# Conversion of 64-bit weights to 32 bits: the exponent test on ScalarE, one mask on VectorE, the integer sum last on GpSimd

## The chip, the cores and the metric

The kernel runs on one core of a Trainium2 chip. The core has a matrix engine (TensorE, in the rows PE, with its weight loads as PEld), VectorE (DVE), ScalarE (ACT), GpSimd (POOL) and SyncE (SP), which issues most DMA transfers. Each engine works through its own queue in order; semaphores tie them together. The metric is the device time of one execution in microseconds, lower is better.

## The reference

Three networks run one after the other: attention with local and global tokens, a top-1 mixture of eight experts, and a gated feed-forward network. The change lies in the preparation of the third one's weights.

```python
def _moe_ref(x, w_gate, w_local, w1, w2):          # the experts
    ...                                            # per token an expert e: its own best, or the one before it
    h = np.maximum(x[b, s] @ w1[e], 0.0)
    out[b, s] = p[e] * (h @ w2[e])

def _moe2_ref(x, w_in, conv_w, w_out):             # the "second network" of the kernel's feed-forward part
    h = np.maximum(x @ w_in, 0.0)
    ...                                            # conv_out: 3 taps of conv_w along the sequence
    gate = 1.0 / (1.0 + np.exp(-conv_out))
    return (h * gate @ w_out).astype(np.float32)
```

`w_in` (512 x 1024), `w_out` (1024 x 512) and `conv_w` (3 x 1024) come as 64-bit floats. The kernel reads each number as two 32-bit words and makes a 32-bit float of it with integer operations: the sign and exponent moved by three bits, the mantissa rounded, and zero where the exponent is too small.

## The kernel before, in words

The order of instructions on every engine is that of the Python code (a manual schedule). After attention, tokens are sorted into slots of at most 128 tokens of one expert. `Moe.run` goes through the slots with `step(s)`; step s does, in this order:

- `layer1(s)`: 24 matmuls of 128x512 into `hp` (the expert's first layer in three products of high and low parts), then two ReLU copies on ACT into `hs`. A slot with few tokens (`few_l1`) uses small matmuls and one short ReLU.
- `fetch(s, 1)`: load of the next first-layer weights if the expert changes. `gather` of the slot after next but one.
- `turn_x(s + 1)`: four transposes on PE (L1353) into `xlp`, ACT's cast to `xh` (L1363), DVE's difference `xl` (L1103).
- the closing operation of the conversion that the step before began (`self.conv.pop()()`, its instruction is L1019 on DVE).
- `raw_load`: SP's load of the next raw chunk (L1481) into one of two halves of `fx`.
- `resplit(s + 1, 1)`: if the expert changes, ACT casts the new weights to `wh` (L1045) and DVE makes `wl` (L1046), inside a branch whose end is L1331. `layer1` of the next slot waits for that end on DVE whether the expert changes or not.
- `convert`, the early place (L1457), if the next slot's expert does not change.
- `layer2(s - 1)`: 24 matmuls into `yp` (L1126), the copy to `ys` on ACT (L1438, or L1413 with few tokens), a scatter on POOL.
- `turn_h(s)`: eight transposes (L1424), two casts to `gh` on ACT (L1425), two differences `gl` on DVE (L1103); with few tokens only L1401 and one copy (L1402).
- `resplit(s, 2)`: the second-layer weights, eight `wh` and eight `wl` of 128x512.
- `convert`, the late place (L1471), if the next slot's expert changes.

So each of the 16 chunks (128 x 512 numbers) is converted once, in steps 3 to 18, early or late; a conversion of `conv_w` (24 x 128 numbers) follows after step 19. Before, a conversion is six DVE operations (L1012 to L1017), a sum on POOL (L1018), and one DVE operation that is put off to the next step (L1019): an XOR and the AND with the exponent test. `wf` holds the converted chunks; they are used when all slots are done (`split`, `split_out`).

Of the kernel before, what the change touches and what calls it, by code (L numbers as in the profile page):

```python
# [8 lines left out]
F32 = mybir.dt.float32  # L9
# [993 lines left out]
POOL_F = ()  # L1003
DVE_F = (1, 3, 5, 7)
POOL_K = {1: (), 2: ()}


def conv64(nc, raw, out):
    hi, lo = raw[:, :, 1], raw[:, :, 0]
    v = nc.vector  # L1010
    a = out.bitcast(I32)
    v.tensor_scalar(a, hi, 3, 0x7FFFFFFF, ALU.logical_shift_left, ALU.bitwise_and)  # L1012
    v.scalar_tensor_tensor(a, hi, -2 ** 31, a, ALU.bitwise_and, ALU.bitwise_or)
    v.tensor_scalar(hi, hi, 1, 21, ALU.logical_shift_left, ALU.logical_shift_right)
    v.tensor_scalar(hi, hi, 897.0, -1.0, ALU.is_ge, ALU.mult)
    v.scalar_tensor_tensor(a, lo, 29, a, ALU.logical_shift_right, ALU.bitwise_or)
    v.tensor_scalar(lo, lo, 28, 1, ALU.logical_shift_right, ALU.bitwise_and)  # L1017
    nc.gpsimd.tensor_tensor(a, a, lo, ALU.add)  # L1018
    return lambda: v.scalar_tensor_tensor(a, a, 0x40000000, hi, ALU.bitwise_xor, ALU.bitwise_and)  # L1019


class Weights:
# [28 lines left out]


class Moe:
    def __init__(self, sig, tc, W, ident, x_dram, y_dram, rt, w1, w2, wi, wo):
        self.nc, self.tc = tc.nc, tc
        self.W, self.ident, self.x_dram, self.y_dram = W, ident, x_dram, y_dram
        self.rt, self.w1, self.w2, self.wi, self.wo = rt, w1, w2, wi, wo
        self.sig = sig
        self.xs, self.xt, self.ht, self.hs, self.next, self.chg, self.sm = {}, {}, {}, {}, {}, {}, {}
        self.conv, self.raw = [], {}  # L1060

    def open(self, ctx):
        self.ctx = ctx
# [123 lines left out]
    def run(self, cw6, cwr, cw, f2):  # L1187
        nc, W, tc = self.nc, self.W, self.tc
        n = NSLOT - 3
        self.f2 = f2  # L1190
        for s in range(NA, n - 1):
            self.step(s)
            if s == NA + 17:
                self.conv.append(conv64(nc, cw6, cwr))
        self.last(n - 1, cwr, cw)
        r = nc.values_load(self.rt.esi[0:1, 4, 1:2], min_val=0, max_val=P + 1)
        with tc.If(r != 0):
            r = nc.values_load(self.rt.esi[0:1, 4, 0:1], min_val=0, max_val=NB)
            with tc.If(r > n - NA):
                for s in range(n, NSLOT):  # L1200
                    self.slot(s)
            f2.load0()
            for i in range(5):
                f2.scale0(i, self.ps)
                f2.xt0(i, self.ps)
        self.split_out()
# [236 lines left out]
    def step(self, s):  # L1443
        W, hi = self.W, NSLOT - 3
        self.small(s + 1)
        self.layer1(s)
        self.fetch(s, 1)
        if s + 3 < hi:
            self.xs[s + 3] = self.gather(s + 3)
        self.turn_x(s + 1)  # L1450
        while self.conv:
            self.conv.pop()()
        if s < NA + 16:
            self.raw_load(s - NA)
        self.resplit(s + 1, 1)
        if NA < s <= NA + 16:
            with self.tc.If(self.chg[s + 1] == 0):  # L1457
                self.convert(s - NA - 1)
        if s == NA:
            for _ in self.rest:  # L1460
                pass
        else:
            self.layer2(s - 1)
            self.fetch(s - 1, 2)
        if s == hi - 2:
            self.f2.load0()
        self.turn_h(s)
        self.resplit(s, 2)
        if NA < s <= NA + 16:
            self.conv.pop()  # L1470
            with self.tc.If(self.chg[s + 1] != 0):  # L1471
                self.convert(s - NA - 1)

# [8 lines left out]

    def convert(self, s):
        n, k, o = self.chunk(s)
        self.conv.append(conv64(self.nc, self.raw[s], self.W.f[n][:, k, o:o + 512]))


class Ffn2:
# [249 lines left out]
def moe_kernel(ctx, tc, q_l, k_l, v_l, q_g, k_g, v_g, w_gate, w_local, w1, w2, w_in, conv_w, w_out, out):  # L1738
    nc = tc.nc
    outf = out.rearrange("b s d -> (b s) d")  # L1740
    with tc.manual_schedule():
# [9 lines left out]
        warm = cp.tile([P, 1], F32, name="warm")  # L1751
        nc.scalar.activation(warm, ident[:, 0:1], AF.Exp)
        L = cp.tile([P, NT, 9], F32, name="L")
        cp.tile([P, PAD_C], F32, name="pad_c")
        cc = Consts()

        def late():
# [22 lines left out]
        def hook(n, end):  # L1780
            if n + end > 20 and (end or todo.get("y") != "pe"):
                for _ in range(STEPS_A[end]):
                    todo["y"] = next(ph, 0)
                    if todo["y"] == "es":
                        todo["load"] = True
                    if todo["y"] in (0, "pe"):
                        break
            if not end:
                return
            if n == N_Y:  # L1790
                nc.sync.dma_start(y_dram[0:S, :], x_dram[0:S, :])
            if n == 25:
                right.close()
                hl = ctx.enter_context(tc.tile_pool(name="w_hl", bufs=1, side="right"))
                st = moe_ctx.enter_context(tc.tile_pool(name="w_x", bufs=1, side="right"))
                W = Weights(nc, hl, st)
                m = todo["m"] = Moe(warm, tc, W, ident, x_dram, y_dram, rt, w1, w2, w_in.bitcast(I32),
                                    w_out.bitcast(I32))
            m = todo.get("m")
            if todo.pop("load", False):  # L1800
                W = m.W
                todo["e0"] = m.reg(nc.sync, 0, 0, E - 1)
                for a in (0, 2):
                    W.load_k(1, w1[bass.ds(todo["e0"], 1)], a, a + 2)
            if m and todo.get("y") == 0 and not m.xs and not m.xt:
                todo["g"] = n
                ca.close()
                todo["xp"] = xa.enter_context(tc.tile_pool(name="m_xa", bufs=1, side="right"))
                for s in range(NA):
                    m.xs[s] = m.gather(s, todo["xp"])  # L1810
            if n - todo.get("g", n) == GATHER_T:
                m.hs0 = todo["xp"].tile([P, FF], F32, name="hs0")
                m.xt[0] = m.hi_lo_t(m.xs.pop(0), NKC, "x", todo["xp"], at.ps)
            for k in SPLIT_W1.get(n, ()):
                m.W.split_k(1, m.W.s, k, nc.gpsimd)
            if n in (30, 31):
                for a in range(2):
                    k = 4 * (n - 30) + 2 * a
                    m.W.load_k(2, w2[bass.ds(todo["e0"], 1)], k, k + 2)
            if n == 32:  # L1820
                cs.close()
                m.psh = moe_ctx.enter_context(tc.tile_pool(name="m_h", bufs=1, space=PSUM, side="right"))
                todo["fill"] = m.fill()
            if n >= 32:
                for _ in range(TAIL[n - 32]):
                    next(todo["fill"])
                for k in SPLIT_W2.get(n, ()):
                    m.W.split_k(2, m.W.s, k, nc.vector)
# [71 lines left out]
```

## Time and profile before

| | us |
|---|---|
| three timed runs | 618.85, 621.88 (median), 623.83 |
| profiled execution, device time | 619.98 |
| its span, first to last instruction | 618.2 |
| PE busy | 571.3 (92% of the span) |
| DVE busy | 407.5 (66%) |
| ACT busy | 308.3 (50%) |
| POOL busy | 173.7 (28%) |

The profile is of one execution. A timeline lists instructions with their start from the first instruction of the program, in microseconds, and in brackets how long the engine was idle before one and what ended that. Matmuls overlap, so their sums exceed the stretch. A windows view gives busy time by engine and the clock that TensorE was granted (1.00 is 2.4 GHz, 0.50 is 1.2 GHz) for stretches of the span.

### The profile page before, as it was taken

To read this page: it belongs to the slowest core of one execution; us is meant where nothing else is said; L and a number is where in the kernel's file an instruction comes from. 1 tells how busy PE (TensorE), PEld (TensorE's weight loads), DVE (VectorE), ACT (ScalarE), POOL (GpSimd) and SP (SyncE) were. 2 spreads that over 40 slices of the span, in tenths; PEclk is the share of its full clock that TensorE was granted. 3 is DMA by queue.
4 is the path that set the end of the run, shared out by engine and by line. 5 is a ranking of instruction groups with operands and counts; after the bars stand their busy time and mean duration, and the time that the engine had idled before them with its cause. 6 is when DMAs were issued, how large, how long until landed. Compare 5 with 4: busy or idle time off the path is not lost. (4 is left out here: it accounts for less than half of the span.)

```text
span 618.2 us, 16382 instructions
## 1 busy us (share of the span) xinstructions
PE 571.3 (92%) x6108; PEld 477.8 (77%) x6108; DVE 407.5 (66%) x854; ACT 308.3 (50%) x623; POOL 173.7 (28%) x226
## 2 busy tenths in 40 slices
PE   7779899888889999989989799979899999999997
PEld 6567677666667888768767688769898998998986
DVE  7868576875974867885687885366864484383330
ACT  5755555565225544652454724547753564463441
POOL 7655830034022423143132431010302313300100
PEclk9998899999999999999999989979899999999999
DMA  9989949568229765576357593322110201000001
GB/s 230 216 184 247 237 114 209 175 216 255 83 64 323 285 228 218 160 282 236 135 177 264 187 319 107 125 83 64 52 36 25 77 18 35 35 0 35 36 35 51
DMA packets 60643, 90.57 MB, mean 147 GB/s; under 512 B 25726, under 2 KB 34198, under 8 KB 60504
## 3 DMA queue, kind: packets, MB, share of 16 engines
q1 hardware_dynamic: 57016, 78.93, 42.1%
q0 software_dynamic: 3520, 10.23, 4.9%
q8 instruction: 65, 1.06, 0.7%
q14 instruction: 42, 0.34, 0.2%
HBM read 125.87 MB, written 15.79 MB: 229 GB/s over the span
## 5 line engine op out<-in xcount | busy, mean ns | idle before, releaser
L1604 DVE SCALAR_TENSOR_TENSOR fc<-f_hp,cw,fc 128x544 f32<-128x544 f32 (+2 forms) x66 | 51.7, 783 | 73.3 <-ACT fc L1602 71.9
L1046 DVE TENSOR_TENSOR wl<-ws,wh 128x512 fp32r<-128x512 f32 (+1 forms) x80 | 64.6, 869 | 8.1 <-ACT wh L1045 6.9
L1045 ACT CAST wh<-ws 128x512 fp32r<-128x512 f32 (+1 forms) x84 | 58.0, 770 | 1.7 <-DMA ws<-in_moe_w_dram 0.7
L1126 PE MATMUL yp<-wh,gh 128*128 128x512 f32 x136 | 54.8, 403 | 0.9 <-ACTq L1331 0.9
L1662 PE MATMUL f<-wh,fh 128*128 128x512 f32 (+1 forms) x144 | 54.8, 381 | 0.0
L1126 PE MATMUL yp<-wl,gh 128*128 128x512 f32 x136 | 53.5, 394 | 1.1 <-DVEq L1331 0.7
L1662 PE MATMUL f<-wh,fl 128*128 128x512 f32 (+1 forms) x144 | 54.4, 378 | 0.0
L1662 PE MATMUL f<-wl,fh 128*128 128x512 f32 (+1 forms) x144 | 54.4, 378 | 0.0
L1126 PE MATMUL yp<-wh,gl 128*128 128x512 f32 x136 | 53.3, 392 | 0.0
L1110 PE MATMUL hp<-wl,xh 128*128 128x512 f32 x136 | 45.5, 407 | 8.4 <-DVEq L1331 5.3
L1083 POOL DMA_INDIRECT y_dram<-ys,sidx x22 | 25.4, 1156 | 86.5 <-ACT ys L1438 38.7
L1309 ACT ACTIVATE hs<-hp 128x512 f32<-128x512 f32 x34 | 18.7, 594 | 61.3 <-PE hp L1110 61.3
L278 ACT ACTIVATE pr<-sp,nm 128x128 f32<-128x128 f32 x128 | 36.6, 376 | 24.7 <-DVE nm L275 24.7
L1110 PE MATMUL hp<-wh,xh 128*128 128x512 f32 x136 | 46.2, 412 | 0.2 <-ACT ys L1413 0.2
L1071 POOL DMA_INDIRECT xs<-x_dram,gidx x22 | 26.9, 1223 | 65.3 <-DMA ws<-in_moe_w_dram 34.0
L1110 PE MATMUL hp<-wh,xl 128*128 128x512 f32 x136 | 44.7, 401 | 0.0
L1018 POOL TENSOR_TENSOR wf<-wf,fx 128x512 int32<-128x512 int32 x16 | 20.9, 1304 | 74.0 <-DVE fx L1017 65.6
L1110 PEld LDWEIGHTS hp<-wl,xh 128*128 128x128 f32 x136 | 25.8, 193 | 15.8 <-DVEq L1331 6.6
L1609 ACT ACTIVATE f_hp<-f 128x544 f32<-128x544 f32 x31 | 19.4, 625 | 37.4 <-PE f L1585 33.4
L1103 DVE TENSOR_TENSOR gl<-hlp,gh 128x512 fp32r<-128x512 f32 x34 | 22.0, 685 | 18.3 <-ACT gh L1425 13.9
L1438 ACT COPY ys<-yp 128x512 f32<-128x512 f32 x15 | 8.9, 591 | 50.0 <-PE yp L1126 47.2
L1671 ACT COPY fy<-f 128x512 f32<-128x512 f32 (+1 forms) x18 | 10.1, 564 | 46.7 <-PE f L1662 46.7
(381 smaller groups left out, 1529.0 us busy)
## 6 DMA issues: line engine op xcount, KB each, us to landing
ws<-in_moe_w_dram SPq DMA_DIRECT2D x42, 2048.0 KB
fx<-y_dram SPq DMA_DIRECT2D x17, 256.0 KB
raw<-in_k_l_dram SPq DMA_DIRECT2D x16, 256.0 KB
x_dram<-x SPq DMA_DIRECT2D x16, 256.0 KB
fx<-in_moe_w_in_dram SPq DMA_DIRECT2D x8, 512.0 KB
fx<-in_moe_w_out_dram SPq DMA_DIRECT2D x8, 512.0 KB
out_dram<-fy SPq DMA_DIRECT2D x16, 256.0 KB
VA<-in_v_l_dram SPq DMA_DIRECT2D x20, 192.0 KB
```

The source lines that it names most:

```text
L278: nc.scalar.activation(pr[:, hp, :], sp[:, hp, :], AF.Exp, bias=nm[:, hp:hp + 1], scale=-1.0)
L1018: nc.gpsimd.tensor_tensor(a, a, lo, ALU.add)
L1045: (cp.tensor_copy if cp else self.nc.scalar.copy)(h, src[n][:, k, :])
L1046: eng.tensor_tensor(l, src[n][:, k, :], h.bitcast(F32), ALU.subtract)
L1071: self.nc.gpsimd.indirect_dma_start(out=xs, out_offset=None, in_=self.x_dram[0:n, :], in_offset=bass.IndirectOffsetOnAxis(ap=self.rt.gidx[ ...
L1083: self.nc.gpsimd.indirect_dma_start(out=self.y_dram[:, :], out_offset=bass.IndirectOffsetOnAxis(ap=self.rt.sidx[:, s:s + 1], axis=0), in_= ...
L1103: self.nc.vector.tensor_tensor(hl[1][:, a:a + 4], t, hl[0][:, a:a + 4].bitcast(F32), ALU.subtract)
L1110: self.nc.tensor.matmul(hp[c], a[:, k, :], b[:, 512 * c:512 * c + 512], start=k == 0 and m == 0, stop=k == NKC - 1 and m == 2)
L1126: self.nc.tensor.matmul(yp, a[:, k, :], b, start=k == 0 and m == 0, stop=k == NFC - 1 and m == 2)
L1604: nc.vector.scalar_tensor_tensor(c[:, a:b], hp[:, a + t:b + t], self.cw[:, t, f:f + 1], c[:, a:b], ALU.mult, ALU.add)
L1609: self.nc.scalar.activation(hp[:, 1:S + 1].rearrange("p (a c) -> p a c", a=2), p[:, :, 0:272], AF.Relu)
L1662: self.nc.tensor.matmul(yp[:, cs], x[:, c], w[:, cs], start=f == 0 and n == 0, stop=f == NFC - 1 and n == 2)
```

## The change

The exponent test goes from DVE to ACT: the high word, read as a 32-bit float, is made positive (`Abs`), compared with the limit `TINY` by `Sign(limit - x)`, and written as an integer: -1, all bits set, where the number is large enough. `m`, one tile for all conversions, is the fifth part of `fx`, which nothing else uses in these steps. On DVE the shift's mask and the sign's mask change their constants, which makes the XOR unnecessary; the two exponent operations go, and one AND of `a` with `m` is added. POOL's sum is the last step, and nothing is put off. The limit stands in a column of a tile that was there as padding.

```diff
@@ -1003,20 +1003,20 @@
-def conv64(nc, raw, out):
+TINY = (9 - 2.0 ** -20) * 2.0 ** -18
+def conv64(nc, raw, out, m, lim):
     hi, lo = raw[:, :, 1], raw[:, :, 0]
-    v = nc.vector
-    a = out.bitcast(I32)
-    v.tensor_scalar(a, hi, 3, 0x7FFFFFFF, ALU.logical_shift_left, ALU.bitwise_and)
-    v.scalar_tensor_tensor(a, hi, -2 ** 31, a, ALU.bitwise_and, ALU.bitwise_or)
-    v.tensor_scalar(hi, hi, 1, 21, ALU.logical_shift_left, ALU.logical_shift_right)
-    v.tensor_scalar(hi, hi, 897.0, -1.0, ALU.is_ge, ALU.mult)
+    v, a, n = nc.vector, out.bitcast(I32), m.shape[0]
+    nc.scalar.activation(m, hi.bitcast(F32), AF.Abs)
+    nc.scalar.activation(m.bitcast(I32), m, AF.Sign, bias=lim[0:n], scale=-1.0)
+    v.tensor_scalar(a, hi, 3, 0x3FFFFFFF, ALU.logical_shift_left, ALU.bitwise_and)
+    v.scalar_tensor_tensor(a, hi, -2 ** 30, a, ALU.bitwise_and, ALU.bitwise_or)
     v.scalar_tensor_tensor(a, lo, 29, a, ALU.logical_shift_right, ALU.bitwise_or)
     v.tensor_scalar(lo, lo, 28, 1, ALU.logical_shift_right, ALU.bitwise_and)
+    v.tensor_tensor(a, a, m.bitcast(I32), ALU.bitwise_and)
     nc.gpsimd.tensor_tensor(a, a, lo, ALU.add)
-    return lambda: v.scalar_tensor_tensor(a, a, 0x40000000, hi, ALU.bitwise_xor, ALU.bitwise_and)
...
@@ -1191,7 +1191,7 @@
             if s == NA + 17:
-                self.conv.append(conv64(nc, cw6, cwr))
+                conv64(nc, cw6, cwr, f2.x_in[4][0:3 * NFC, 0:P], self.lim)
...
@@ -1448,8 +1448,6 @@
         self.turn_x(s + 1)
-        while self.conv:
-            self.conv.pop()()
         if s < NA + 16:
             self.raw_load(s - NA)
...
         if NA < s <= NA + 16:
-            self.conv.pop()
             with self.tc.If(self.chg[s + 1] != 0):
                 self.convert(s - NA - 1)
...
     def convert(self, s):
         n, k, o = self.chunk(s)
-        self.conv.append(conv64(self.nc, self.raw[s], self.W.f[n][:, k, o:o + 512]))
+        conv64(self.nc, self.raw[s], self.W.f[n][:, k, o:o + 512], self.f2.x_in[4], self.lim)
...
-        cp.tile([P, PAD_C], F32, name="pad_c")
+        lim = cp.tile([P, PAD_C], F32, name="pad_c")[:, 0:1]
+        nc.vector.memset(lim, TINY)
```

Line numbers in the order of the changed kernel: L1012 and L1013 are the two ACT operations, L1014 to L1018 DVE's five, L1019 POOL's sum; L1455 is the early place (L1457 before), L1468 the late one (L1471 before).

DVE, from the transposes of the next slot to the branch on its first-layer weights, before:

```order
L1340 UNCONDITIONAL_BRANCH x2
L1340 COMPARE_AND_BRANCH
L1340 UNCONDITIONAL_BRANCH
L1103 TENSOR_TENSOR xl<-xlp,xh 128x512
L1340 UNCONDITIONAL_BRANCH
L1019 SCALAR_TENSOR_TENSOR wf_3966<-wf_3966,fx 128x512
L1324 TENSOR_LOAD esi
L1331 COMPARE_AND_BRANCH
```

and now:

```order
L1340 UNCONDITIONAL_BRANCH x2
L1340 COMPARE_AND_BRANCH
L1340 UNCONDITIONAL_BRANCH
L1103 TENSOR_TENSOR xl<-xlp,xh 128x512
L1340 UNCONDITIONAL_BRANCH
L1324 TENSOR_LOAD esi
L1331 COMPARE_AND_BRANCH
```

`xl` is followed directly by the register load and the branch; the put-off operation on `wf` is gone.

DVE, the early place of a conversion, before:

```order
L1457 COMPARE_AND_BRANCH
L1012 TENSOR_SCALAR wf_3966<-fx 128x512
L1013 SCALAR_TENSOR_TENSOR wf_3966<-fx,wf_3966 128x512
L1014 TENSOR_SCALAR fx<-fx 128x512
L1015 TENSOR_SCALAR fx<-fx 128x512
L1016 SCALAR_TENSOR_TENSOR wf_3966<-fx,wf_3966 128x512
L1017 TENSOR_SCALAR fx<-fx 128x512
L1457 UNCONDITIONAL_BRANCH x2
```

and now:

```order
L1455 COMPARE_AND_BRANCH
L1014 TENSOR_SCALAR wf_3967<-fx 128x512
L1015 SCALAR_TENSOR_TENSOR wf_3967<-fx,wf_3967 128x512
L1016 SCALAR_TENSOR_TENSOR wf_3967<-fx,wf_3967 128x512
L1017 TENSOR_SCALAR fx<-fx 128x512
L1018 TENSOR_TENSOR wf_3967<-wf_3967,fx 128x512
L1455 UNCONDITIONAL_BRANCH x2
```

Two operations on `fx` (the raw high word) are gone from the middle, an AND on `wf` stands at the end.

ACT, from the last of the `wh` casts of the next first-layer weights to the copies of the second layer's result, before:

```order
L1045 CAST wh_3_2731<-ws_3447 128x1024
L1331 UNCONDITIONAL_BRANCH x2
L1457 COMPARE_AND_BRANCH
L1457 UNCONDITIONAL_BRANCH x2
L1340 COMPARE_AND_BRANCH
```

and now:

```order
L1045 CAST wh_3_2732<-ws_3448 128x1024
L1331 UNCONDITIONAL_BRANCH x2
L1455 COMPARE_AND_BRANCH
L1012 ACTIVATE fx<-fx 128x512
L1013 ACTIVATE fx<-fx,pad_c 128x512
L1455 UNCONDITIONAL_BRANCH x2
L1340 COMPARE_AND_BRANCH
```

The two activations stand between the casts and the `ys` copies. At the late place they stand in the same way behind the `wh` casts of the second layer and ahead of the next slot's ReLU. PE's instructions and those of POOL and SP are the same in the same order.

## Rows read from the trace of the kernel before

**Rows 1.** The page's first line: span and instructions of the profiled execution.
```profile
span 618.2 us, 16382 instructions
```

**Rows 2.** Timeline of PE: start us, busy us, engine, line, operation, count, [idle before, releaser].
```profile
276.81 0.98 PE L1110 MATMUL hp<-wl,xh 128*128 128x512 f32 x2 [2.12 <-DVEq L1331]
...
283.52 0.60 PE L1353 MATMUL xlp<-ident,xs 128*128 128x128 f32 x4
...
322.55 0.73 PE L1110 MATMUL hp<-wl,xh 128*128 128x512 f32 x2 [2.10 <-DVEq L1331]
...
327.68 0.60 PE L1353 MATMUL xlp<-ident,xs 128*128 128x128 f32 x4
...
355.45 1.09 PE L1110 MATMUL hp<-wl,xh 128*128 128x512 f32 x2 [3.14 <-DVE wl L1046]
...
362.17 0.60 PE L1353 MATMUL xlp<-ident,xs 128*128 128x128 f32 x4
```

**Rows 3.** Timeline of DVE ahead of the first of these.
```profile
263.25 0.69 DVE L1103 TENSOR_TENSOR xl<-xlp,xh 128x512 fp32r<-128x512 f32 x1 [0.63 <-issue]
264.04 0.69 DVE L1019 SCALAR_TENSOR_TENSOR wf<-wf,fx 128x512 int32<-128x512 int32 x1
265.14 0.43 DVE L1012 TENSOR_SCALAR wf<-fx 128x512 int32<-128x512 int32 x1 [0.41 <-DVEq L1331]
265.60 0.69 DVE L1013 SCALAR_TENSOR_TENSOR wf<-fx,wf 128x512 int32<-128x512 int32 x1
266.33 0.43 DVE L1014 TENSOR_SCALAR fx<-fx 128x512 int32<-128x512 int32 x1
266.79 0.43 DVE L1015 TENSOR_SCALAR fx<-fx 128x512 int32<-128x512 int32 x1
267.14 0.69 DVE L1016 SCALAR_TENSOR_TENSOR wf<-fx,wf 128x512 int32<-128x512 int32 x1
267.86 0.43 DVE L1017 TENSOR_SCALAR fx<-fx 128x512 int32<-128x512 int32 x1
268.85 5.61 DVE L1046 TENSOR_TENSOR wl<-ws,wh 128x512 fp32r<-128x512 f32 x8 [0.56 <-PE hp L1110]
275.41 0.69 DVE L1103 TENSOR_TENSOR xl<-xlp,xh 128x512 fp32r<-128x512 f32 x1 [0.95 <-ACTq L1331]
276.01 0.68 DVE L1019 SCALAR_TENSOR_TENSOR wf<-wf,fx 128x512 int32<-128x512 int32 x1
276.93 0.43 DVE L1012 TENSOR_SCALAR wf<-fx 128x512 int32<-128x512 int32 x1 [0.23 <-DVEq L1331]
```

**Rows 4.** Windows: length, busy of PE, PEld, DVE, ACT, POOL; granted clock; DMA; GB/s.
```profile
276.80:283.50 6.70, 6.69 (x22) 5.33 (x23) 4.29 (x8) 0.00 (x0) 2.33 (x2) 0.75 0.83 255
...
322.50:327.70 5.20, 5.15 (x23) 4.21 (x24) 4.30 (x8) 0.00 (x0) 1.64 (x2) 1.00 0.73 230
```

**Rows 5.** Timeline of DVE ahead of the second and third.
```profile
309.31 0.69 DVE L1103 TENSOR_TENSOR xl<-xlp,xh 128x512 fp32r<-128x512 f32 x1 [0.91 <-issue]
...
310.90 0.43 DVE L1012 TENSOR_SCALAR wf<-fx 128x512 int32<-128x512 int32 x1 [0.23 <-DVEq L1331]
...
341.01 0.69 DVE L1103 TENSOR_TENSOR xl<-xlp,xh 128x512 fp32r<-128x512 f32 x1 [0.63 <-issue]
...
342.73 0.43 DVE L1012 TENSOR_SCALAR wf<-fx 128x512 int32<-128x512 int32 x1 [0.23 <-DVEq L1331]
```

**Rows 6.** Timeline of ACT around the first.
```profile
264.84 0.59 ACT L1438 COPY ys<-yp 128x512 f32<-128x512 f32 x1 [5.03 <-PE yp L1126]
...
271.39 0.57 ACT L1363 CAST xh<-xlp 128x512 fp32r<-128x512 f32 x1
272.88 1.06 ACT L1413 COPY ys<-yp 32x128 f32<-32x128 f32 x4 [0.92 <-PE yp L1410]
```

**Rows 7.** Line 1541 on ACT: count, shortest, median and longest ns, first and last start.
```profile
L1541 ACT ACTIVATE fx<-fx,gate x5: 708/711/727, 421.5 to 433.7; 128x512 f32<-128x512 f32 x5
```

**Rows 8.** Timeline of SP: issue of a raw chunk's load.
```profile
264.75 0.35 SPq L1481 DMA_DIRECT2D fx<-in_moe_w_in_dram  x1
```

More of the change, by code (lines that the diff above doesn't have):

```diff
@@ L1053, with __init__ @@
 class Moe:
-    def __init__(self, sig, tc, W, ident, x_dram, y_dram, rt, w1, w2, wi, wo):
+    def __init__(self, sig, lim, tc, W, ident, x_dram, y_dram, rt, w1, w2, wi, wo):
         self.nc, self.tc = tc.nc, tc
@@ L1057, in __init__ @@
         self.rt, self.w1, self.w2, self.wi, self.wo = rt, w1, w2, wi, wo
-        self.sig = sig
+        self.sig, self.lim = sig, lim
         self.xs, self.xt, self.ht, self.hs, self.next, self.chg, self.sm = {}, {}, {}, {}, {}, {}, {}
-        self.conv, self.raw = [], {}
+        self.raw = {}
     def open(self, ctx):
@@ L1796, in hook @@
                 W = Weights(nc, hl, st)
-                m = todo["m"] = Moe(warm, tc, W, ident, x_dram, y_dram, rt, w1, w2, w_in.bitcast(I32),
+                m = todo["m"] = Moe(warm, lim, tc, W, ident, x_dram, y_dram, rt, w1, w2, w_in.bitcast(I32),
                                     w_out.bitcast(I32))
```

## The prediction

> **What bounds the kernel now.** I read the span first [rows 1], then TensorE's timeline where it stands still while conversions run, then the queue of the engine that ends each standstill. A conversion of a weight chunk is never waited for as such: its result is used only by the second network's splits, behind the last slot. It costs time where its instructions stand in an engine's queue ahead of something that TensorE needs. [rows 2] show the three places in that stretch where TensorE is idle for more than a few tenths: 2.12 us before 276.81, 2.10 before 322.55, 3.14 before 355.45. All three end with VectorE (DVE), and each stands in the step after one with a small expert (few tokens, no `gl` work). [rows 3] show the queue behind the first: the `xl` of one slot, the conversion's closing operation (L1019), six operations of the next conversion, eight `wl` differences (L1046), the next `xl`, another closing operation at 276.01, and at 276.81 TensorE goes on. DVE is behind, and I read no pause in it as caused by another engine: the 0.56 and 0.95 us before `wl` and `xl` lie where its order has only branches and register loads, whatever releaser the view names for them. TensorE waits for the end of the branch at L1331, and L1019 at 276.01 stands in front of it. So here DVE's queue is the path, and what is taken out of it moves the end.
>
> A second loss hangs on the first. From 276.81 to the next transposes at 283.52 TensorE takes 6.71 us, from 322.55 to 327.68 the same 24-matmul layer takes 5.13, and from 355.45 to 362.17 6.72 [rows 2]. The granted clock is 0.75 in the first of these stretches and 1.00 in the second [rows 4]: a part at 1.2 GHz after the stall, all at 2.4 GHz in the other. The price of such a fall is 6.71 − 5.13 = 1.6 us, and it came behind two of three stalls.
>
> **The change, part by part.** *DVE, the conversion's own operations.* Removed are two single-source operations on the exponent, moved to ScalarE (ACT); added is one AND with two inputs. Pitches from [rows 3]: shift 0.46 (265.14 to 265.60), sign 0.73 (to 266.33), the first exponent operation 0.46, the second 0.35, the low word's OR 0.72 (267.14 to 267.86), the low word's shift 0.43: 3.15 in all. Now: 0.46 + 0.73 + 0.72 + 0.35 for the shift, which the AND need not wait for, + the AND itself. That last is not in the trace as such; bounds are 0.43 (one input) and 0.69 (two inputs and a constant), and I take 0.68, since `wl` and the closing operation read two inputs too. Sum 2.94: 0.2 less for each conversion.
>
> *DVE, the closing operation.* It disappears. At the first stall it costs twice. Between `xl` at 263.25 and the next conversion lie 1.89 us; without it `xl` itself (0.69) and the 0.24 of branch that follow such an operation stay, so 0.96 go, the wait for GpSimd's sum in it included. At 276.01 it starts as `xl` ends; TensorE's release moves from its end to `xl`'s: 0.6. The other two places: from `xl` to the conversion 1.59 (309.31 to 310.90) and 1.72 (341.01 to 342.73) [rows 5], less 0.93, so 0.66 and 0.79; and 0.6 each behind the last `xl`, by the row at 276.01.
>
> *Sum on DVE.* Two conversions and two closing operations lie ahead of each stall. First 0.2 + 0.96 + 0.2 + 0.6 = 2.0 of 2.12; second 0.2 + 0.66 + 0.2 + 0.6 = 1.7 of 2.10; third 0.2 + 0.79 + 0.2 + 0.6 = 1.8 of 3.14, which leaves 1.3 there because four wide `wl` of the next weights follow. Together 5.5 us. The closing operation and the 0.2 at the other ten conversions are hidden: TensorE is fed there by `xl`, `gl` and `wl` that are done before it asks, so they are worth nothing.
>
> *ACT.* It gets 16 pairs of 128x512, and one of 24x128. The nearest rows are `xh`, 0.57 [rows 6], and an activation with a per-partition operand, 0.71 [rows 7]; I take 0.6 for the magnitude, which has no such operand, and 0.7 for the sign, 1.3 for a pair. From below a pair takes 2 x 0.57 = 1.1; from above, if reading every second word halved ACT's rate, 2.6 (DVE's strided read at 265.14 shows no such loss [rows 3], so I stay near the lower end). Cover: ahead of the `ys` copy at 264.84, which waits for TensorE, ACT stands idle 5.03 us [rows 6]. Both 1.3 and 2.6 fit. A new wait ties them: there is one scratch tile, so the magnitude of a conversion waits for the AND of the one before. At the first stall that AND ends about 259.5 + 2.9 = 262.4 by the 2.94 above (the conversion ahead starts 3.15 + 0.63 before `xl` at 263.25 [rows 3]), the pair then ends at 263.7, ahead of 264.84 and ahead of the next AND (about 266). Queued behind ACT's pair are the `ys` copies and `gh` casts; one step later the pair stands between `xh` (ends 271.96) and the copies at 272.88 [rows 6] and pushes these by some 0.4; the reader of the casts, `gl`, stands on DVE behind the whole conversion that starts at 276.93 [rows 3], so it costs nothing.
>
> *GpSimd and the queues.* The sum starts as before behind DVE's last operation. The load of the next raw chunk on SyncE, at 264.75 right behind the closing operation [rows 8], is let go by the sum instead, about a microsecond earlier. No DMA is added. The one-column memset at the start is under 0.3 and nothing waits for it.
>
> *A rule against it.* For copies and simple arithmetic the Trainium skill (ScalarE: Activation LUTs, Rules for kernel authors) says to use VectorE, not ScalarE. The rows agree on the engines' own time: 0.9 leave DVE for each conversion and 1.3 come to ACT. By that count the change would cost 16 x 0.4 = 6 us of engine time; by the queue that TensorE waits for it gains. I go by the queue, because ACT has the idle 5.03.
>
> *Clock.* Of the three stalls 0.1, 0.4 and 1.3 us stay. The 2.10 us stall kept its clock, so I expect that these do too: two falls of 1.6 go, 3.2 us. Bounds: none goes (0), or the falls move elsewhere.
>
> *Total.* 5.5 + 3.2 = 8.7. The profiled execution's own time is 619.98, 1.8 more than its span [rows 1]: 611.3. The median of the three timed runs is 621.88, with 618.85 to 623.83; the mean of the four executions is 621.1, which gives 612.4. I say 612.
>
> **The rivals.** *The clock stays as it is* (the shorter stalls still cost it, or it falls elsewhere): only 5.5 go, 614.5 against 620.0, 615.6 against 621.1. For it: two of three stalls had a fall. Against: the one without was 2.10 long, more than any that I expect to remain.
>
> *The wait changes its name.* DVE's AND waits for ACT's sign, or the `wl` stay bound by something that I take for branches; what DVE saves comes back as a wait and the stalls stay. Time 619 to 621. For it: the new chain magnitude, sign, AND, sum runs over three engines, and one scratch tile couples neighbours. Against: by the times above the sign is ready 2 us before the AND.
>
> *Slower: ACT blocks on a raw load.* ACT reads the raw chunk in order, ahead of copies that free TensorE's results. It comes to it at 271.96, 7.2 us after the load at 264.75 was issued; DVE read it at 276.93 without a wait, 12.2 after [rows 3, 6, 8]. A load that lands more than 7.2 + 5.0 − 1.3 = 10.9 us after its issue makes the `ys` copy late, each microsecond beyond that is TensorE's, at most 1.3 by the 12.2. At nine conversions of this position: 12 us, about 632. Against it: the load is issued about a microsecond earlier now, and the rows leave only the stretch from 10.9 to 12.2 for it.
>
> *Slower by table switches.* Every ACT operation of the change could need something loaded ahead of it that the program does not show. If that cost as much again as each operation and its partner, the pair's 1.3 would become 3.9; begun at 262.4 it would end at 266.3, 1.5 behind the copy at 264.84 and TensorE with it. At half of the 16 conversions that is 12 us, about 632. Against it: the order of the change's instructions has no further table load on ACT. The Trainium skill (ScalarE: Activation LUTs, Table sets: the hidden batching unit) tells of such switches; it lists the magnitude as filler of every set and does not name the sign.
>
> **How the numbers follow.** Forecast, stalls shorter and at least one fall of the clock gone (609 to 614): 0.58. Clock unchanged (614.5 to 615.6): 0.15. Wait renamed (619 to 621): 0.17. ACT blocked: 0.07. Tables: 0.03. A measurement of this kernel can tell about 1% from no change, 6 us. Faster by over 1%, under 614 to 615: 0.58. Within: the clock and renamed cases, 0.32. Slower by over 1%: 0.10. The range reaches from 608.5, one more fall gone, up to 618.5; it leaves out the two slower cases and part of the renamed one. The likeliest one's own range is 609 to 614.
>
> **What would show it.** Right: the idle time before `hp` in the three steps after small experts is 0 to 0.5, 0 to 0.8 and 1 to 1.6 us; the layer behind each takes 5.1 to 5.3 us at granted clock 1.00; the pair on ACT takes 1.2 to 1.5 and nothing of TensorE waits for it; no `ys` copy starts later than TensorE's `yp` by more than 0.5. Wrong: DVE's AND idle for ACT; ACT's magnitude idle for a DMA; a stall of more than 2 us at any of the three; or the same stalls gone and the time still above 616, which would mean that the time came back behind the conversions, in the loads and splits ahead of the second network.

## The result and the profile after

The changed kernel takes 611.34 us (median, 610.01 to 613.47); the kernel before takes 621.36 beside it (618.85 to 623.83). The ratio is 0.9853, with a 95% interval of 0.981 to 0.9895. The forecast was 612.0. (The ratios here and below use only runs in the faster of the two states that executions fall into, and are not the quotient of the two medians.)

The profiled execution of the changed kernel has a device time of 611.46 us. Two lines of its page, the span and the busy times of the engines:

```profile
span 609.7 us, 16446 instructions
...
PE 570.2 (94%) x6108; PEld 478.0 (78%) x6108; DVE 393.5 (65%) x821; ACT 331.0 (54%) x657; POOL 170.6 (28%) x226
```

Against [rows 1] the span is 8.5 us shorter. DVE lost 14.0 us of work and ACT got 22.7. By busy time alone the change would be a loss of 8.7 us.

The three places of [rows 2] in the changed kernel, from the timeline of PE (start us, busy us, engine, line, operation, count, [idle before, releaser]). The transposes (L1353) mark where one step ends and the next begins:

```profile
271.05 0.60 PE L1353 MATMUL xlp<-ident,xs 128*128 128x128 f32 x4
...
275.02 0.70 PE L1110 MATMUL hp<-wh,xh 128*128 128x512 f32 x2 [0.27 <-PE hlp L1424]
275.56 0.64 PE L1110 MATMUL hp<-wl,xh 128*128 128x512 f32 x2
...
280.59 0.60 PE L1353 MATMUL xlp<-ident,xs 128*128 128x128 f32 x4
...
313.45 0.60 PE L1353 MATMUL xlp<-ident,xs 128*128 128x128 f32 x4
...
317.96 0.73 PE L1110 MATMUL hp<-wl,xh 128*128 128x512 f32 x2
...
323.09 0.60 PE L1353 MATMUL xlp<-ident,xs 128*128 128x128 f32 x4
...
343.54 0.60 PE L1353 MATMUL xlp<-ident,xs 128*128 128x128 f32 x4
...
348.83 0.73 PE L1110 MATMUL hp<-wl,xh 128*128 128x512 f32 x2 [0.65 <-DVE wl L1046]
...
353.94 0.60 PE L1353 MATMUL xlp<-ident,xs 128*128 128x128 f32 x4
```

The waits of 2.12, 2.10 and 3.14 us ahead of `hp<-wl,xh` are 0, 0 and 0.65 now. A windows view of the three layers behind them, with the columns of [rows 4]:

```profile
275.50:280.60 5.10, 5.10 (x24) 4.17 (x24) 4.04 (x7) 2.85 (x8) 1.57 (x2) 1.00 0.91 314
317.90:323.10 5.20, 5.20 (x24) 4.20 (x24) 4.04 (x7) 2.02 (x6) 1.58 (x2) 1.00 0.95 311
348.80:354.00 5.20, 5.17 (x23) 4.25 (x24) 4.58 (x5) 4.09 (x10) 1.01 (x1) 1.00 1.02 352
```

The granted clock is 1.00 in all three. Before, the first and the third had fallen to half speed for a part; [rows 4] show the first, and this is the third:

```profile
355.40:362.20 6.80, 6.75 (x23) 5.36 (x24) 5.81 (x7) 0.26 (x2) 0.88 (x1) 0.75 0.92 299
```

The most useful measure turned out to be the length of these three steps, from the transposes of one slot to those of the next. In the kernel before, the steps start with these rows of PE's timeline and end with the L1353 rows of [rows 2]:

```profile
270.31 0.60 PE L1353 MATMUL xlp<-ident,xs 128*128 128x128 f32 x4
...
316.26 0.60 PE L1353 MATMUL xlp<-ident,xs 128*128 128x128 f32 x4
...
348.10 0.60 PE L1353 MATMUL xlp<-ident,xs 128*128 128x128 f32 x4
```

So the first step took 283.52 − 270.31 = 13.21 us and takes 280.59 − 271.05 = 9.54. Each of the other 16 steps is as long in one kernel as in the other, within 0.13 us (seven of them take 12.29 in both). The same measure for the kernels of the next section, each from its own L1353 rows (the line number moves by a few). It is worked out from unrounded starts, so a last digit can differ by 0.01 from the rows:

| kernel | first | second | third | sum | median us |
|---|---|---|---|---|---|
| before | 13.21 | 11.41 | 14.07 | 38.70 | 621.36 |
| after | 9.54 | 9.64 | 10.40 | 29.58 | 611.34 |
| after, a second profile | 9.53 | 9.63 | 10.43 | 29.59 | 611.27 |
| E1 closing operation in front, all on DVE | 11.03 | 10.94 | 13.87 | 35.84 | 618.33 |
| E2 test on ACT, closing operation put off | 9.83 | 9.84 | 10.72 | 30.39 | 610.88 |
| E3 after, the AND twice | 11.40 | 11.15 | 13.67 | 36.21 | 617.43 |
| E8 before, PE kept busy | 11.59 | 11.42 | 12.44 | 35.45 | 614.37 |
| E4 after, two more ACT operations | 9.56 | 9.47 | 10.41 | 29.44 | 609.72 |
| E6 after, one DVE operation left | 9.32 | 9.11 | 9.10 | 27.53 | 608.53 |

The kernel before, run beside them, took 621.34 us (median) for E1 to E4, 619.10 for E5, E6, E7 and the second run of the changed kernel, and 619.62 for E8.

38.70 − 29.58 = 9.12 us come from the three steps. The profiled span fell by 8.5; the rest, 0.6, is lost outside them, mostly ahead of the first. What lies ahead of the first of these steps (267.3 to 273.7 us over all kernels run) and behind the last transposes (229.1 to 231.5) differs between executions. Some of that is not the kernel's: the first of these transposes, ahead of any conversion, start between 176.25 us (E4) and 182.96 (E5). So a median moves by some microseconds on its own.

### The profile page after: what moved, and what is told of

The parts are those of the page before. It is cut to its first block, busy times and chain, and to the rows that moved or that the text cites. A ratio compares the mean times of both kernels' runs of the same rounds, so it can differ in the third digit from the quotient of the medians.

```text
span 609.7 us, 16446 instructions
## 1 busy us (share of the span) xinstructions
PE 570.2 (94%) x6108; PEld 478.0 (78%) x6108; DVE 393.5 (65%) x821; ACT 331.0 (54%) x657; POOL 170.6 (28%) x226
## 5 line engine op out<-in xcount | busy, mean ns | idle before, releaser
L1110 PE MATMUL hp<-wl,xh 128*128 128x512 f32 x136 | 43.8, 394 | 1.7 <-DVEq L1331 1.1
L1071 POOL DMA_INDIRECT xs<-x_dram,gidx x22 | 25.3, 1151 | 70.7 <-ACT pr L278 34.0
L1019 POOL TENSOR_TENSOR wf<-wf,fx 128x512 int32<-128x512 int32 x16 | 20.9, 1308 | 60.0 <-DVE wf L1018 54.7
L1659 PEld LDWEIGHTS f<-wh,fl 128*128 128x128 f32 x144 | 27.1, 188 | 5.1
```

The lines of the kernel that those rows point to most:

```text
L1071: self.nc.gpsimd.indirect_dma_start(out=xs, out_offset=None, in_=self.x_dram[0:n, :], in_offset=bass.IndirectOffsetOnAxis(ap=self.rt.gidx[ ...
L1110: self.nc.tensor.matmul(hp[c], a[:, k, :], b[:, 512 * c:512 * c + 512], start=k == 0 and m == 0, stop=k == NKC - 1 and m == 2)
L1659: self.nc.tensor.matmul(yp[:, cs], x[:, c], w[:, cs], start=f == 0 and n == 0, stop=f == NFC - 1 and n == 2)
```

## The experiments

The theory: TensorE waits at three places for the end of DVE's queue; the change takes about 2 us out of that queue at each, and the two falls of the clock go with the waits. Rivals: what counts is only that the closing operation no longer stands ahead of the branch (E1, E2); the chain over three engines costs something that hides in the gain (E4, E6); the clock is a bystander (E8).

**E1: the closing operation in front, everything on DVE.** From the kernel before. Nothing goes to ACT and nothing is put off; DVE keeps the exponent test and closes with an AND ahead of POOL's sum.

```diff
-    v.tensor_scalar(a, hi, 3, 0x7FFFFFFF, ALU.logical_shift_left, ALU.bitwise_and)
-    v.scalar_tensor_tensor(a, hi, -2 ** 31, a, ALU.bitwise_and, ALU.bitwise_or)
+    v.tensor_scalar(a, hi, 3, 0x3FFFFFFF, ALU.logical_shift_left, ALU.bitwise_and)
+    v.scalar_tensor_tensor(a, hi, -2 ** 30, a, ALU.bitwise_and, ALU.bitwise_or)
...
+    v.tensor_tensor(a, a, hi, ALU.bitwise_and)
     nc.gpsimd.tensor_tensor(a, a, lo, ALU.add)
-    return lambda: v.scalar_tensor_tensor(a, a, 0x40000000, hi, ALU.bitwise_xor, ALU.bitwise_and)
```

> Only the place of the closing operation changes against the kernel before: the exponent test stays on VectorE, the AND stands ahead of GpSimd's sum, nothing is put off. A conversion becomes seven VectorE operations, 3.15 + 0.6 = 3.75 us, and the put-off operation (0.66 to 0.96 and 0.6 us ahead of each stall) goes. Theory (the length of VectorE's queue ahead of each stall decides): per stall 2 x 0.6 come and 1.3 to 1.6 go, so the stalls of 2.12, 2.10 and 3.14 us become 1.8, 2.0 and 2.9; the clock falls about as before; 618 to 621 us. Rival (what counts is that nothing stands between xl and the branch that TensorE waits for): the stalls shrink as in the change, 612 to 614 us.

618.33 us (615.82 to 621.72), ratio 0.997 (0.9943 to 0.9996). PE's waits, from its timeline, and the windows of the first and third layer:

```profile
277.66 0.72 PE L1110 MATMUL hp<-wl,xh 128*128 128x512 f32 x2 [1.61 <-DVEq L1331]
...
321.36 0.73 PE L1110 MATMUL hp<-wl,xh 128*128 128x512 f32 x2 [1.63 <-DVEq L1331]
...
354.05 1.15 PE L1110 MATMUL hp<-wl,xh 128*128 128x512 f32 x2 [2.92 <-DVE wl L1046]
```
```profile
277.60:282.80 5.20, 5.14 (x22) 4.19 (x23) 4.63 (x9) 0.00 (x0) 0.94 (x1) 1.00 0.98 341
354.00:360.70 6.70, 6.65 (x22) 5.34 (x23) 5.61 (x7) 0.46 (x1) 0.88 (x1) 0.75 0.92 317
```

The waits stay, within 0.4 us of what the theory gave. Moving the closing operation is worth 0.2 to 0.6 us a step; the further 1.6 in the first step is the clock, which held behind 1.61 us of idle time and fell behind 2.92. That is 2.86 of the 9.12 us of the change; the rest needs the work off DVE.

**E2: the test on ACT, the closing operation put off as before.** From the changed kernel; the rest as in the kernel before.

```diff
-    v.tensor_tensor(a, a, m.bitcast(I32), ALU.bitwise_and)
     nc.gpsimd.tensor_tensor(a, a, lo, ALU.add)
+    return lambda: v.tensor_tensor(a, a, m.bitcast(I32), ALU.bitwise_and)
...
```

> The other half alone: the exponent test on ScalarE as in the change, but the AND is put off to the next step, behind xl and ahead of the branch, as the kernel before has it. A conversion is four VectorE operations, 2.34 us, plus the put-off one. Theory (length of the queue): 0.8 go from each of two conversions ahead of a stall, 1.6 per stall, so 0.5, 0.5 and 1.5 us of stall stay, no fall of the clock: 612 to 615 us. Rival (the place of the closing operation counts): the stalls stay near 2 us or more, 618 to 621 us.

610.88 us (608.57 to 615.38), ratio 0.9845 (0.9806 to 0.9884).

```profile
275.45 0.50 PE L1110 MATMUL hp<-wl,xh 128*128 128x512 f32 x1 [0.40 <-DVEq L1331]
...
318.15 0.50 PE L1110 MATMUL hp<-wl,xh 128*128 128x512 f32 x1 [0.52 <-DVEq L1331]
...
349.32 0.50 PE L1110 MATMUL hp<-wl,xh 128*128 128x512 f32 x1 [1.38 <-DVE wl L1046]
```

The time is a little below what was expected (612 to 615). The waits are the theory's, 0.5, 0.5 and 1.5, and no fall of the clock lies in the stretch. With the closing operation put back where it was, nearly all of the gain stays: its three steps are 0.29, 0.20 and 0.32 us longer than in the changed kernel, 0.8 in sum. The medians of the two can't be told apart. So E1 and E2 together say: the length of DVE's queue decides. The place of the last operation is worth 0.2 to 0.6 us a step, and in the kernel before one fall of the clock besides (E1).

**E3: the AND twice.** The changed kernel with one more 128x512 operation in each conversion.

```diff
     v.tensor_tensor(a, a, m.bitcast(I32), ALU.bitwise_and)
+    v.tensor_tensor(a, a, m.bitcast(I32), ALU.bitwise_and)
```

> The changed kernel with the AND on VectorE done twice (same result), 0.68 us more per conversion. Theory: two conversions stand ahead of each stall, so each grows by 1.4 us, to some 1.6, 1.6 and 2.0; the other ten conversions hide it; 4 us from the stalls and 0 to 3.3 from falls of the clock: 615 to 619 us. Rival (the gain came from elsewhere, for instance from GpSimd or from the earlier raw loads): no change, 611 to 612 us.

617.43 us (613.77 to 621.74), ratio 0.9951 (0.9923 to 0.9979).

```profile
276.25 0.50 PE L1111 MATMUL hp<-wl,xh 128*128 128x512 f32 x1 [2.00 <-DVEq L1332]
...
320.26 0.50 PE L1111 MATMUL hp<-wl,xh 128*128 128x512 f32 x1 [1.83 <-DVEq L1332]
...
352.79 0.63 PE L1111 MATMUL hp<-wl,xh 128*128 128x512 f32 x1 [2.75 <-DVE wl L1047]
```
```profile
352.70:359.50 6.80, 6.71 (x22) 5.32 (x23) 5.71 (x8) 2.50 (x5) 1.74 (x1) 0.75 0.95 334
```

The time lies where it was expected, the waits are 0.2 to 0.75 longer than that. Two more operations, each 0.72 us from its start to the next one's, stand ahead of each wait, 1.44; the steps grew by 1.86, 1.51 and 3.27, the last with a fall of the clock behind the wait, which the window shows (3.27 − 1.6 = 1.6). The excess in the first comes with a longer gap ahead of `xl` there (0.67 us, against 0.36 and 0.37 at the other two places), which the last section takes up. 0.7 us of DVE work in a conversion costs 6.6 us in these three steps: 16 x 0.7 = 11 us of work, of which the three places show only the two conversions ahead of each, and one fall.

**E8: PE kept busy through the waits.** The kernel before, with 16 transposes of the identity into an unused part of `yp`, in slots with few tokens ahead of their second layer. No work is taken from DVE.

```diff
+NFILL = 16
...
+        def few():
+            for i in range(NFILL if s >= 6 else 0):
+                nc.tensor.transpose(yp[:, 128 + 128 * (i % 3):256 + 128 * (i % 3)], self.ident, self.ident)
+            self.few_l2(hs, yp, y)
...
```

> The kernel before with the 16 transposes ahead of the second layer of the slots with few tokens, where their target is not yet read by ScalarE (behind it, they waited for ScalarE's copies and then delayed TensorE). VectorE's queue is unchanged. Theory (the stall and the clock behind it are two losses): TensorE comes to the wait 1.8 us later and waits 0.2 to 1.4 instead of 2.1 to 3.1; the layer behind each takes 5.1 to 5.4 us, no stretch at 0.50 there: 617 to 619.5 us, against some 621 of the kernel before. Rival (the slow stretch comes with the place, not with the idle time): layers of 6.7 behind the first and the third, 620 us or more.

614.37 us (611.69 to 617.29) beside 619.62, ratio 0.9909 (0.988 to 0.9937): a larger gain than expected (617 to 619.5). PE's timeline, and the windows of the first and the third layer:

```profile
272.45 1.91 PE L1443 MATMUL yp<-ident 128*128 128x128 f32 x16
274.29 1.95 PE L1411 MATMUL yp<-ws,hs 128*32 128x128 f32 x64
...
278.49 0.73 PE L1111 MATMUL hp<-wl,xh 128*128 128x512 f32 x2 [0.53 <-DVEq L1332]
...
322.63 0.50 PE L1111 MATMUL hp<-wl,xh 128*128 128x512 f32 x1 [0.33 <-DVEq L1332]
...
355.55 0.50 PE L1111 MATMUL hp<-wl,xh 128*128 128x512 f32 x1 [1.44 <-DVE wl L1047]
```
```profile
278.40:283.60 5.20, 5.11 (x22) 4.19 (x23) 4.29 (x8) 0.09 (x1) 1.61 (x2) 1.00 0.81 225
355.50:360.60 5.10, 5.05 (x22) 4.19 (x23) 4.48 (x5) 0.29 (x1) 0.88 (x1) 1.00 0.91 292
```

The 1.84 us of transposes (272.45 to 274.29) only fill the waits: the layer starts no earlier. Where the clock had fallen, the step is shorter, by 1.62 and 1.63; where it had not, it is the same (11.42 against 11.41). That is the price of a fall, measured by itself, and equal to the 1.6 of the forecast. So of the 9.12 us of the change 3.25 are clock and 5.87 are shorter waits. E8's median gained 5.3, 2 us more than the three steps explain. In its profile the stretch ahead of the first step is 1.7 us longer than before and the one behind the last transposes 2.4 shorter (229.1 us, 231.5 before). The experiment touches neither, so the 2 us can't be tied to it.

**E4: two more ACT operations.** The changed kernel, with the magnitude taken three times.

```diff
     nc.scalar.activation(m, hi.bitcast(F32), AF.Abs)
+    nc.scalar.activation(m, m, AF.Abs)
+    nc.scalar.activation(m, m, AF.Abs)
```

> The changed kernel with two more magnitudes in place on ScalarE in each conversion, about 1.4 us more of ScalarE for each of 16. Theory (ScalarE has the time while it waits for TensorE's second layer): within 1 us of the changed kernel, 610.5 to 612.5 us. Rival (ScalarE is now close to the path, in front of the ys copies and gh casts): it pays at some or all of the 16, 614 to 634 us.

609.72 us (605.63 to 615.18), ratio 0.9834 (0.9796 to 0.9873); sum of the three steps 29.44 against 29.58. Twenty microseconds more of ACT (351.4 busy) cost nothing in these steps, so the pair of the change costs nothing there either. The pair's place in the queue is not what anything waits for. The median is a little below what was expected (610.5 to 612.5).

**E6: one DVE operation left.** The changed kernel with only the first DVE operation of each conversion; the exponent test, the sign, the low word and the sum are left out, so the weights of the second network are unfinished.

```diff
-    nc.scalar.activation(m, hi.bitcast(F32), AF.Abs)
...
-    nc.gpsimd.tensor_tensor(a, a, lo, ALU.add)
+    nc.vector.tensor_scalar(out.bitcast(I32), hi, 3, 0x3FFFFFFF, ALU.logical_shift_left, ALU.bitwise_and)
```

> The changed kernel with all but the first VectorE operation of each conversion left out (no magnitude, no sign, no further VectorE operations, no sum on GpSimd), so the second network gets unfinished weights. Theory: the conversions of the changed kernel cost at most the 1.3 us of idle time that TensorE still has in that stretch: 609.5 to 612 us. Rival (they still cost time that no stall shows, by ports or by traffic): 606 us or less.

608.53 us (607.42 to 612.54), ratio 0.9841 (0.9795 to 0.9886): 1 us below what the theory gave (609.5 to 612) and not the 606 or less of the rival. The three steps are 2.05 us shorter than in the changed kernel, 1.30 of it in the third. That is all that the conversions, but for one operation each, still cost in these steps: what was to be had there is mostly had.

**The changed kernel once more**, beside E5, E6 and E7.

> The changed kernel itself, for comparison in the same call: 610 to 613 us, stalls of 0 to 0.3, 0 to 0.3 and 0.6 to 1.1 us behind the slots with few tokens, no fall of the clock there.

611.27 us (609.11 to 613.01), ratio 0.9873 (0.9829 to 0.9918). Its second profile has the same steps within 0.03 us, but waits of 0.30 and 1.08 us where the first shows 0 and 0.65: the step's small matmuls ran earlier, and the layer started at the same place in it. A wait can move within a step; the step's length is the firmer number.

**E5: PE kept busy, in the wrong place.** The same transposes as in E8, behind the few-token second layer.

```diff
+NFILL = 16
...
+        def few():
+            self.few_l2(hs, yp, y)
+            for i in range(NFILL if s >= 6 else 0):
+                nc.tensor.transpose(yp[:, 128 + 128 * (i % 3):256 + 128 * (i % 3)], self.ident, self.ident)
...
```

> The kernel before with 16 transposes of the identity (about 1.8 us, results unused) on TensorE behind the second layer of each slot with few tokens from slot 6 on, so that TensorE is busy where it would stand still ahead of the three stalls. VectorE's queue is unchanged. Theory (stall and fall of the clock are two losses, and the second follows from the idle time): the layer behind each stall starts when it did, and takes 5.1 to 5.3 us instead of 6.7 in two of three cases: 617 to 619 us. Rival (the clock falls whatever TensorE does there, or the slow stretch has another cause): the layers stay at 6.7, 620 to 622 us, or more if the transposes cost time.

621.83 us (617.94 to 627.1), ratio 1.0037 (0.9999 to 1.0074). The design failed: the transposes write a buffer that ACT's copy still reads, so they made a wait of their own.

```profile
277.42 1.97 PE L1444 MATMUL yp<-ident 128*128 128x128 f32 x16 [1.20 <-ACT ys L1414]
```

In the third step that wait was 4.03 us long, with a fall behind it. It says nothing on the clock; E8 was made for that.

**E7: the clock kept to the end.** The changed kernel, with fillers of 5 to 16 transposes (54 in all) in the gaps ahead of and in the second network.

```diff
+        wm = self.y_tile()
...
+        def keep(n):
+            for i in range(n):
+                nc.tensor.transpose(wm[:, P * (i % 4):P * (i % 4) + P], self.ident, self.ident)
...
+        keep(6)
...
```

> The changed kernel with transposes of the identity on TensorE (results unused) in the idle places between the last slot and the second network (6, 5, 8, 13 and 6 of them) and ahead of the one-time wait in the second network (16). Theory (idle time costs the clock behind it): the stretches at 0.50 that follow there, 6.83 and 3.41 us in the trace of the changed kernel, go or shorten: 607 to 610 us. Rival (the clock follows something else): 611 to 613 us.

609.92 us (607.88 to 614.44), ratio 0.9855 (0.9807 to 0.9904). That lies inside the 607 to 610 that were expected, but it can't be told from the changed kernel beside it (611.27). One line of its page (granted clock in 40 slices, 9 is 90% or more; the mean over the execution is 1.000) and a row of PE's timeline:

```profile
PEclk9999999999999999999999999999999999999999
```
```profile
414.74 0.52 PE L1594 MATMUL f<-f_x0h,wh 128*128 128x272 f32 x2 [1.65 <-ACT f_hp L1618]
```

The clock did not fall at all, and the time hardly moved. The wait for ACT in the row is new: in the changed kernel PE has none over 0.25 us in that part of the second network. That suggests that a part of what the falls cost came back as waits for another engine; how much is not shown. None of the kernels here beats the changed one by more than the measurement can tell.

## Why the prediction was right, and where its terms were not

**The place and the mechanism.** Right. The gain lies in the three named steps; no other step moved by more than 0.13 us. Per step the forecast had 2.0 + 1.6, 1.7, and 1.8 + 1.6; measured are 3.67, 1.77 and 3.67. In sum: 8.7 forecast, 9.12 measured. That the median (611.34) came within 0.7 us of the forecast (612.0) is closer than the method can promise, since a median moves by more than that on its own.

**The clock.** Two falls of 1.6 were to go and did (E8: 1.62 and 1.63). The expectation that waits shorter than the 2.10 us that had kept its clock would keep theirs held in each kernel run: in this stretch falls stand at waits of 2.12, 2.75, 2.92, 3.14 and 4.03 us, and none at 2.10, 2.00, 1.83, 1.63, 1.61 or less. It is no rule on the length of a wait: 2.10 and 2.12 went either way, and ahead of the second network the changed kernel's clock falls at shorter ones. There PE waits 0.93 us before 394.24, 0.73 before 396.25, 1.10 before 399.30 and 1.68 before 402.04, and the granted clock is at half (a windows view of the changed kernel, columns as in [rows 4]):

```profile
401.70:408.50 6.80, 5.59 (x22) 4.88 (x23) 5.16 (x10) 2.82 (x6) 1.25 (x7) 0.50 0.12 20
```

**DVE's queue: the sum was right, two of its terms were not.** DVE's timeline of the changed kernel at the first place, to be held against [rows 3]:

```profile
262.17 0.43 DVE L1017 TENSOR_SCALAR fx<-fx 128x512 int32<-128x512 int32 x1
262.51 0.69 DVE L1018 TENSOR_TENSOR wf<-wf,fx 128x512 int32<-128x512 int32 x1
263.23 0.69 DVE L1103 TENSOR_TENSOR xl<-xlp,xh 128x512 fp32r<-128x512 f32 x1
264.55 0.43 DVE L1014 TENSOR_SCALAR wf<-fx 128x512 int32<-128x512 int32 x1 [0.63 <-DVEq L1331]
...
268.11 5.62 DVE L1046 TENSOR_TENSOR wl<-ws,wh 128x512 fp32r<-128x512 f32 x8 [0.55 <-ACT wh L1045]
274.67 0.69 DVE L1103 TENSOR_TENSOR xl<-xlp,xh 128x512 fp32r<-128x512 f32 x1 [0.94 <-ACTq L1331]
```

- *Ahead of `xl`* the forecast had 0.2 us, the conversion that is shorter by that. Against the transposes of its step `xl` starts 0.85, 0.70 and 0.80 us earlier at the three places. The idle 0.63, 0.91 and 0.63 ahead of `xl` [rows 3, 5] is gone: the AND runs in that time. The forecast priced the AND at 0.68 (measured 0.684) and did not see that it fits where DVE's branches and register loads stood bare.
- *From `xl` to the next conversion* the forecast took out 0.96, 0.66 and 0.79. The first was 1.89 and is 264.55 − 263.23 = 1.32, so 0.57; the others 0.21 (1.38 left of 1.59) and 0.64 (1.08 left of 1.72). The step that failed is that "`xl` itself (0.69) and the 0.24 of branch that follow such an operation stay". The closing operation had covered part of the branches' time; without it 0.39 to 0.69 us of branch are visible, not 0.24.
- *The second conversion and the release* are as forecast: 0.15 at the first place and 0.14 at the second for the 0.2, and 0.59 for the 0.6 at the second (from `xl` to `hp`, 322.55 − 321.15 = 1.40 before, 317.96 − 317.15 = 0.81 now). At the third both together give 0.60 for 0.8.

By place: 2.1, 1.6 and 2.0 where 2.0, 1.7 and 1.8 were forecast. The two misses are one fact seen twice: branch time is hidden or bare depending on what stands next to it. They nearly cancel; that was luck. The prediction's remark that the pauses in DVE's queue are branches and not waits for others fits: ahead of `wl` and `xl` they are as long in the changed kernel (0.55 and 0.94 us) as before (0.56 and 0.95), whatever releaser the view names. These pauses should have been priced as terms.

**ACT.** The changed kernel, by line: the magnitude with its durations, what it was idle for, and who waited for it.

```profile
L1012 ACT ACTIVATE fx<-fx x16: 660/680/717, 200.4 to 357.6; 128x512 f32<-128x512 f32 x16
...
  DVE wf L1018: 9.8, 5
...
  DMA fx<-in_moe_w_in_dram: 0.9, 1
...
who waited for it (us, times):
  DVE xl L1103: 0.9, 1
  PEld hp L1110: 0.2, 1
```

The pair takes 0.68 + 0.724 = 1.40, not 1.3, and far from the 2.6 of the upper bound. (The prediction read from [rows 3] that a strided read costs DVE nothing; all one-source operations there are strided, so those rows have nothing to compare with.) No table load shows up around it: each kernel has two on ACT, at 0.73 and 399.89 us before and at 0.73 and 391.60 now, outside the conversions. The Trainium skill's section that the prediction cites on this (ScalarE: Activation LUTs, Table sets: the hidden batching unit) does name the sign, in its list of precision budgets, but places it in no set. The scratch tile does couple neighbours: five times the magnitude waited for the AND of the conversion ahead, 9.8 us in all, at most 2.3, in time that ACT had. The two waits that the view puts on the magnitude are not its doing: `xl`'s 0.94 us (at 317.15) is the pause of branches that the other two places have as well (0.94 and 0.93), and PE goes on at 317.30 without a pause behind the weight load's 0.2 (at 317.27).

By engine time the change loses 8.7 us (the forecast's count had 6); E4 shows that ACT's time is free here, so that count did not decide. The Trainium skill (ScalarE: Activation LUTs, Rules for kernel authors) says to use VectorE and not ScalarE for `relu`, `max`, `min`, `add` and `mul`; the copies that the prediction adds to them are not in that rule.

**The rival that came close.** ACT did wait for a raw load once, as the slower rival had it, and the prediction counted that among the signs of being wrong. ACT's timeline there:

```profile
274.86 0.66 ACT L1012 ACTIVATE fx<-fx 128x512 f32<-128x512 f32 x1 [0.87 <-DMA fx<-in_moe_w_in_dram]
275.55 0.72 ACT L1013 ACTIVATE fx<-fx,pad_c 128x512 int32<-128x512 f32 x1
276.30 1.06 ACT L1413 COPY ys<-yp 32x128 f32<-32x128 f32 x4
```

The load was issued at 264.63 and let the magnitude go 10.2 us later; the forecast's limit was 10.9. That limit was wrong: its 5.0 us of cover is ACT's idle time ahead of the copy at 264.84, and the copy behind this pair, at 272.88 in [rows 6], has 0.92. So the copy was late at 10.2 already. The load goes out 0.95 us earlier in its step than before (5.27 us behind the transposes at 259.36, where [rows 8] has 6.22 behind those at 258.53); issued as late as before, it would have held ACT for 0.95 us more. What was wrong with the rival is its price: a late copy costs TensorE nothing here. The `ys` copy at 276.30 starts some 2.6 us behind the small matmuls that feed it (271.57 to 273.73), and the layer at 275.56 runs without a wait. In E4 the same copy starts 4.1 us behind its matmuls (267.80 to 269.76), and the step is as long (9.56 us against 9.54):

```profile
273.82 1.06 ACT L1415 COPY ys<-yp 32x128 f32<-32x128 f32 x4
```

So the sign that no `ys` copy starts later than `yp` by more than 0.5 did not come, and it was a bad one to look for: in the kernel before, the third place already had a copy 2.9 us behind, as harmless.

**The signs.** Waits of 0 to 0.5, 0 to 0.8 and 1 to 1.6 were forecast: 0.27 (at the layer's first matmul), 0 and 0.65 in the first profile, 0.30 and 1.08 at the last two in the second. Layers of 5.1 to 5.3 us at granted clock 1.00: 5.03, 5.13 and 5.11. DVE's AND never waited for ACT. Nothing came back behind the conversions: from the last transposes to the end it is 231.5 us before and 231.2 after.

## What to carry to other kernels

Price a moved operation in the queue that is waited for, at the places where it is waited for, not by the engines' busy time: here 0.9 us less for DVE at each of 16 conversions was worth 9 us in three steps and nothing in the others, and 1.4 us more for ACT was free. Measure such a change by the length of the steps, which in the two profiles of the changed kernel agree within 0.03 us at the three places, and take falls of the clock as a term of their own. Count branches and register loads of a queue as a term too: an operation beside them may cost nothing, and taking one away may give back less than it took.

## What the runs showed of the hardware

**Branches run under queued operations, but not always.** In the changed kernel DVE's sequencer takes up the branch behind the conversion at 262.19, when L1017 has just started (262.17) and the AND has not (262.51); from there to `xl` it takes 1.04 us, and the AND lies inside. In the kernel before, it takes it up at 262.20, also with the start of L1017, which is the last operation there:

```profile
262.19 0.43 DVE L1017 TENSOR_SCALAR fx<-fx 128x512 int32<-128x512 int32 x1
```

so the same 1.05 us (to 263.25) stand bare for 0.63. In E3, with the second AND as the last operation, the branch comes at 262.16 with the start of that AND (262.15), and 0.67 us are bare again; at the other two places of E3 it is 0.36 and 0.37, what 1.05 less the AND's 0.69 would leave. Why the first is 0.3 longer stays open. The Trainium skill (Perfetto Trace Analysis, DVE / Act Engine Instruction) says that the sequencer pushes an instruction into a wait queue and is then ready for the next; the changed kernel agrees, while in the other two the sequencer came to the branch only as the last operation started. What may tell the cases apart is whether the last operation depends on the one just ahead of it on DVE. The changed kernel's AND does not, and it starts before that one ends (262.51 against 262.60); nor does E1's, which has no such gap either. In the kernel before the last operation overwrites the low word that the one ahead of it reads, in E2 as well (0.63 us bare again), and in E3 it reads what the one ahead of it writes. No run was made to test this reading.

**Magnitude and sign on ACT.** At 128x512 the magnitude takes 0.680 us from every second word of the raw chunk; from contiguous words, in E4, it takes 0.632:

```profile
L1013 ACT ACTIVATE fx<-fx x17: 310/632/635, 197.4 to 370.4; 128x512 f32<-128x512 f32 x16, 24x128 f32<-24x128 f32 x1
```

So a stride of two costs ACT 0.05 us here, not half its rate. The sign, with a per-partition limit and an integer output, takes 0.724, close to the 0.711 of [rows 7], and no pause lies between the two functions.
